# Second half's model-dimension product by seven block products, and another written order of the pieces around it

## The chip, the cores and the metric

The kernel runs on one NeuronCore of a Trainium2 chip. The metric is device time in microseconds of one execution, as the median of runs. The engines that matter here are TensorE (PE in the profile; weight loads are PEld), VectorE (DVE), ScalarE (ACT), GpSimd (POOL), and SyncE (SP), which only issues transfers here; GpSimd issues transfers too. Data live in SBUF, which the kernel cuts into pages, in PSUM, where matmuls add up, and in device memory.

## The reference, cut to what matters

```python
def _A_ref(x, dft_seq_re, dft_seq_im, dft_hid_re, dft_hid_im):
    a = jnp.einsum("bsd,ed->bse", x, dft_hid_re)
    b = jnp.einsum("bsd,ed->bse", x, dft_hid_im)
    return jnp.einsum("ts,bse->bte", dft_seq_re, a) - jnp.einsum("ts,bse->bte", dft_seq_im, b)

def _B_ref(x, w1, w2):
    h = jnp.einsum("bsd,df->bsf", x, w1)
    h = _silu(h)
    return jnp.einsum("bsf,fd->bsd", h, w2)

h = x + _A_ref(_layernorm(x, axis=-1), A_dft_seq_re, A_dft_seq_im, A_dft_hid_re, A_dft_hid_im)
h2 = h + _B_ref(_layernorm(h, axis=-1), B_w1, B_w2)
```

The sequence has 2048 positions, the model dimension is 512, the hidden one of the feed-forward part 1792, all in float32. So there are two big kinds of products in the first part, along the sequence (2048 by 2048) and along the model dimension (512 by 512), each with a real and an imaginary matrix, and two in the second part.

## The kernel before, in words

Each float32 operand is split into a rounded high part and a remainder, and each product is made of three matmuls, high by high, high by remainder, remainder by high (`three`, lines 199 to 203). The splitting is the preparation: ScalarE rounds (line 151), VectorE subtracts (line 155, or 157 where the operand changes its sign); `rounded` returns the first and leaves the second to be called later.

The kernel takes the sequence product first, because the two dimensions commute, in two halves of the output (q = 0, 1) and with two matrices (c = 0 real, 1 imaginary): `plain(0, 0)`, `fast(1, 0)`, then `mix(0)` along the model dimension, then `fast(0, 1)`, `fast(1, 1)`, `mix(1)`, then the feed-forward part, `up` and `down`, for each half. `fast` (line 543) is a product by seven block products, Strassen's scheme in Winograd's form: matrices cut into 2 by 2 blocks, sums of blocks on the operands, seven products in place of eight, sums of the products. Its product n is worked over four chunks `jj`, 12 matmuls each. The order is 1, 3, 2, then 6, 5, 7 and 4 in turns. `after1` to `after3` (lines 565 to 575) copy finished products out of PSUM on ScalarE, `post` (line 614) adds products up on VectorE. `mix(q)` (line 674) is not by seven products: for each c and each of two halves i of the model dimension and two pieces tau of the output, one step of 24 matmuls with the weights `hid`, which are loaded, rounded and used in each half anew. At its end `add_y` adds the result to the input, `h`, and `store_h` and `norm_h` follow.

All work is written as pieces with a time: `step` puts a block of matmuls at the planner's clock, which counts 0.2265 us a matmul, its preparations at that time less a lead (`LOAD_US` 18 for loads, `PREP_US` 8 for remainders, 2.2 more for the rounding), and what follows it at its end; `at` places other pieces. `program` returns the pieces sorted by these times, and they are written in that order. For the engines in `ORDERED` (PE, DVE, ACT and POOL) the order of writing is held with `issue_after`; the place of SyncE's transfers among themselves is left to the framework. The times are thus an order on each engine, not times at which something starts: an instruction starts when its engine reaches it and its inputs and its output's space are there. A page of SBUF (51 of them, 4 KB a partition) is given to each new tile by `Plan.places`, which takes, in the order of writing, the page whose last use is planned to end first. A load into a page waits for that use.

The sums of the second weights, `make_w2` (line 943), and of the first, `sums_w1` (line 811), are prepared during the first part and kept in device memory, from where `fetch_w2` and `fetch_w1` bring them back.

Of the kernel before, what the change touches and what calls it, by code (L numbers as in the profile page):

```python
# [7 lines left out]
F32 = mybir.dt.float32  # L8
# [59 lines left out]
class Plan:  # L68
# [64 lines left out]
def program(nc, page, keep, small, psum, dram, x, xT, seq, hid, ffn, out):  # L133
# [83 lines left out]
    def at(t, f):  # L217
        events.append((t, 1, len(events), f))
# [113 lines left out]

    cd = [dram.tile([2, 2, P, 2, 512], F32, name=f"cd{q}") for q in range(2)]

    def store_c(q, i, tau):
        nc.gpsimd.dma_start(cd[q][i, tau], C.pop((0, q, i, tau)))

    def load_c(q, i, tau):
        t = C[0, q, i, tau] = page(f"c{q}{i}{tau}")
        nc.sync.dma_start(t, cd[q][i, tau])  # L340

    def begin(keys):

# [34 lines left out]
    def plain(c, q):  # L378
# [154 lines left out]
            step(12, lambda n=n, jj=jj: prod(n, jj), before, after)  # L533
        at(clock[0] + 8, ready)
        for n, v in enumerate(((0, 0), (1, 0), (1, 1), (0, 1))):
            at(clock[0] + 8 + 1.2 * n, lambda v=v: store_c(q, *v))
# [6 lines left out]
    def fast(c, q):  # L543

        A = {1: (0, 0), 2: (0, 1), 3: ("S", 4), 4: (1, 1), 5: ("S", 1), 6: ("S", 2), 7: ("S", 3)}
        B = {1: (0, 0), 2: (1, 0), 3: (1, 1)}

        def mul(n, jj, on=False):
            hi, lo = part.pop(("A", c, q, n, jj))
            w = X[(*A[n], jj)]  # L550
            for m in range(2):
                for a in range(2):
                    d = slice(m * P, (m + 1) * P)
                    three(acc[c, q, n][:, m, :], w[:, 0, a, d], w[:, 1, a, d], hi[:, a, :], lo[:, a, :],
                          jj == JJ[0] and a == 0 and not on, jj == JJ[-1] and a == 1, on)

        kept = {}

        def copy_out(n, name):
            t = kept[name] = page(f"{name}{c}{q}")  # L560
            for m in range(2):
                nc.scalar.activation(t[:, m, :], acc[c, q, n][:, m, :], AF.Copy)
            return t

        def after1():
            copy_out(1, "p1")
            acc[c, q, 2] = acc[c, q, 1]

        def after2():
            C[c, q, 0, 0] = copy_out(2, "c11")  # L570
            acc.pop((c, q, 1)), acc.pop((c, q, 2))

        def after3():
            copy_out(3, "p3")
            acc.pop((c, q, 3))

        for n in (1, 3, 2):
            for jj in JJ:
                key = ("A", c, q, n, jj)

                def mm(n=n, jj=jj):
                    if n != 2 and jj == JJ[0]:
                        acc[c, q, n] = banks(f"m{c}{q}{n}")
                    mul(n, jj, on=n == 2)

                last = jj == JJ[-1]
                step(12, mm, [(LOAD_US, lambda n=n, jj=jj, key=key: load_seq(c, q, jj, *B[n], key)),
                              *halves(PREP_US, lambda key=key: round_raw(key))],
                     [(0, {1: after1, 2: after2, 3: after3}[n])] if last else ())

        def sub(o, a, b):
            nc.vector.tensor_tensor(o, a, b, op=ALU.subtract)  # L592

        B4 = {}

        def load(jj):
            for k, tau in ((0, 1), (0, 0), (1, 1)):
                load_seq(c, q, jj, k, tau, ("B", k, tau))
                B4[k, tau, jj] = raw.pop(("B", k, tau))

        def prep(n, jj):

            b11, b12, b22 = (B4[k + (jj,)] for k in ((0, 0), (0, 1), (1, 1)))
            o = {5: b11, 7: b12, 6: b22, 4: b22}[n]
# [7 lines left out]
            raw["A", c, q, n, jj] = o  # L612

        def post(n):
            if n == 6:
                u2 = kept["p1"]
                nc.vector.tensor_tensor(u2, u2, acc.pop((c, q, 6)), op=ALU.subtract)
                nc.vector.tensor_tensor(kept["p3"], kept["p3"], u2, op=ALU.add)
            elif n == 5:
                t = C[c, q, 0, 1] = kept.pop("p3")  # L620
                nc.vector.tensor_tensor(t, acc[c, q, 5], t, op=ALU.add)
            elif n == 7:
                u3 = kept["p1"]
                nc.vector.tensor_tensor(u3, acc.pop((c, q, 7)), u3, op=ALU.add)
                t = C[c, q, 1, 1] = page(f"c22{c}{q}")
                nc.vector.tensor_tensor(t, acc.pop((c, q, 5)), u3, op=ALU.add)
            else:
                t = C[c, q, 1, 0] = kept.pop("p1")
                nc.vector.tensor_tensor(t, acc.pop((c, q, 4)), t, op=ALU.add)

        for n, j in ((6, 0), (5, 0), (7, 0), (6, 1), (4, 0), (5, 1), (7, 1), (6, 2), (4, 1), (5, 2), (7, 2), (6, 3), (4, 2),
                      (5, 3), (7, 3), (4, 3)):
            jj = JJ[j]

            def mm(n=n, jj=jj):
                if jj == JJ[0]:
                    acc[c, q, n] = banks(f"m{c}{q}{n}")
                mul(n, jj)

            before = halves(ADD_US[1] if n == 4 else PREP_US, lambda k=("A", c, q, n, jj): round_raw(k))  # L640
            if n == 4:
                before.append((ADD_US[0], lambda jj=jj: prep(4, jj)))
            elif n == 6:
                before += [(PREP_US + 2 * GAP_US + d, lambda jj=jj, m=m: prep(m, jj)) for d, m in ((2.4, 5), (1.2, 7), (0, 6))]
                before.append((LOAD_US + 2.4, lambda jj=jj: load(jj)))
            step(12, mm, before, [(0, lambda n=n: post(n))] if jj == JJ[-1] else ())
        if c == 0:
            t = clock[0]
            for i, tau, d in ((0, 0, 0), (0, 1, 2), (1, 0, 8), (1, 1, 8)):
                at(t + d, lambda i=i, tau=tau: store_c(q, i, tau))  # L650


    H, y, h = {}, {}, {}
# [2 lines left out]
        raw["H", c, i] = page(f"hid{c}{i}")  # L656
        nc.sync.dma_start(raw["H", c, i], hid[c, i].rearrange("p (m e) -> p m e", m=2))

    def load_h(q, tau):
        for e in range(2):  # L660
            t = h[q, tau, e] = page(f"h{q}{tau}{e}")
            nc.sync.dma_start(t, xT[2 * tau + q][:, 2 * e : 2 * e + 2, :])

    hd = [dram.tile([2, 2, P, 2, 512], F32, name=f"hd{q}") for q in range(2)]

# [4 lines left out]
    def store_h(q, tau):  # L670
        for e in range(2):
            nc.gpsimd.dma_start(hd[q][tau, e], h[q, tau, e])

    def mix(q):
        for c in range(2):
            for i in range(2):
                for tau in range(2):

                    def round_h(c=c, i=i):
                        H[c, i], remainder = rounded(raw.pop(("H", c, i)), f"H{c}{i}")  # L680
                        return remainder

                    def round_c(tau=tau, c=c, i=i):
# [3 lines left out]

                    def mm(tau=tau, c=c, i=i):
                        hi, lo = part.pop(("M", q, tau, c, i))
                        wh, wl = H[c, i] if tau == 0 else H.pop((c, i))  # L690
# [9 lines left out]
                    if tau == 0:  # L700
                        before = [(LOAD_US, lambda c=c, i=i: load_hid(c, i)), *halves(PREP_US, round_h)] + before
                    if c == 0:
                        before.append((LOAD_US - 1, lambda i=i, tau=tau: load_c(q, i, tau)))
                    if c == 1 and i == 1:
                        before.append((LOAD_US - 6, lambda tau=tau: load_h(q, tau)))
                        after = [(0, lambda tau=tau: add_y(q, tau)), (0.5, lambda tau=tau: store_h(q, tau))]
                    step(24, mm, before, after)
        for tau in range(2):
            norm_h(q, tau, clock[0] + NORM_US[q][tau])
# [431 lines left out]
    for _ in range(WARM):  # L1141
        nc.tensor.matmul(idle[:, 0, :], warm[:, :P], warm, start=True, stop=True)  # L1142

    return sorted(events, key=lambda v: v[:3])


# [32 lines left out]
```

## Time and profile before

| | |
|---|---|
| median of 3 runs | 676.83 us (676.39 to 676.86) |
| profiled execution, its span | 674.5 us |
| TensorE, VectorE, ScalarE, GpSimd busy | 669.2, 556.7, 351.0, 92.0 us |
| matmuls | 2940 |
| transfers | 177.01 MB, 262 GB/s over the span |
| granted clock of TensorE | 1.00 |

The profile is one execution on the chip. Its span runs from the first to the last instruction; the time of a run has some 2.3 us more around it. A line like L155 is a line of the kernel, and `out<-in` names tiles. In rows of groups the numbers after the count are busy time, mean duration of one in ns, and idle time of the engine just before, with what ended it. Where one helper makes all roundings, they share its line, and the tile's name tells them apart: `raw` and `ph`, `pl` for sequence matrices, `c` for the sequence product's result, `hid` and `H..` for the model matrices, `T` for the operands of `up`.

### The profile page before, as it was taken

The page shows a single profiled execution, that of the slowest core. Times are in us where ns is not written, and L with a number is a line of the kernel's source. Part 1 is how long each engine was busy: PE and PEld are TensorE (multiplying, and loading weights), DVE is VectorE, ACT ScalarE, POOL GpSimd, SP SyncE. Part 2 cuts the span into 40 slices and gives each one's busy share as a digit, 9 for nine tenths or more (in the row PEclk, how much of TensorE's full clock was granted, in tenths as well). Part 3 has the DMA queues.
Part 4 walks back from the last instruction along what each step waited for, and adds up shares of the span by engine and source line. Part 5 has one row for each costly group of instructions (what it writes and reads, how often), then busy time and mean ns, then how long its engine had stood idle before and what let it go on. Part 6 is the DMA issues. An engine that isn't in the chain of part 4 may idle for free.

```text
span 674.5 us, 8322 instructions
## 1 busy us (share of the span) xinstructions
PE 669.2 (99%) x2940; PEld 551.2 (82%) x2940; DVE 556.7 (83%) x705; ACT 351.0 (52%) x445; POOL 92.0 (14%) x114
## 2 busy tenths in 40 slices
PE   9999999999999999999999999999999999999997
PEld 6888888888888888888888888888888888888886
DVE  7899999988646899989899989657999555549984
ACT  6789747544422544364454626556654545565510
POOL 0011211110000241123120304511100000000000
PEclk9999999999999999999999999999999999999999
DMA  8968999976599467987799995537997676467702
GB/s 315 397 211 175 310 374 368 274 206 227 188 356 332 166 156 187 339 315 236 219 264 403 414 419 188 197 99 269 387 409 249 214 272 243 187 249 282 280 33 93
DMA packets 58010, 177.01 MB, mean 262 GB/s; under 512 B 6512, under 2 KB 14192, under 8 KB 57968
## 3 DMA queue, kind: packets, MB, share of 16 engines
q1 hardware_dynamic: 44880, 131.09, 53.9%
q0 software_dynamic: 12800, 45.12, 22.2%
q8 instruction: 23, 0.38, 0.2%
q10 hardware_dynamic: 288, 0.26, 0.1%
q14 instruction: 19, 0.16, 0.1%
HBM read 137.63 MB, written 38.81 MB: 262 GB/s over the span
## 4 chain that ended last, share of the span: by engine, by line
PE 99%; DVE 0%; ACT 0%; issue 0%
PE m L202 11%; PE m L201 11%; PE m L203 11%; PE y L201 8%; PE y L203 8%; PE y L202 8%; PE f L203 6%; PE f L201 6%; PE f L202 6%; PE c L203 4%; PE c L201 4%; PE c L202 3%; PE vx L201 3%; PE vx L203 3%; PE vx L202 3%; PE idle L1142 1%
## 5 line engine op out<-in xcount | busy, mean ns | idle before, releaser
L151 ACT ACTIVATE ph<-raw 128x1024 fp32r<-128x1024 f32 x102 | 104.0, 1052 | 106.7 <-DVE raw L592 36.5
L155 DVE TENSOR_TENSOR pl<-raw,ph 128x1024 fp32r<-128x1024 f32 x100 | 124.5, 1258 | 15.0 <-ACT ph L151 14.4
L201 PE MATMUL m<-ph,S 128*128 128x512 f32 x192 | 74.7, 389 | 0.0
L202 PE MATMUL m<-pl,S 128*128 128x512 f32 x192 | 74.7, 389 | 0.0
L203 PE MATMUL m<-ph,S 128*128 128x512 f32 x192 | 74.7, 389 | 0.0
L878 DVE TENSOR_TENSOR g<-vx,g 128x512 f32<-128x512 f32 x42 | 28.8, 688 | 53.6 <-PE vx L203 24.3
L201 PE MATMUL f<-gth,wf 128*128 128x512 f32 x161 | 62.6, 389 | 0.0
L202 PE MATMUL f<-gtl,wf 128*128 128x512 f32 x161 | 62.6, 389 | 0.0
L203 PE MATMUL f<-gth,wf 128*128 128x512 f32 x161 | 62.6, 389 | 0.0
L151 ACT ACTIVATE gth<-g 128x1024 fp32r<-128x1024 f32 x42 | 43.2, 1055 | 36.1 <-DVE g L995 35.0
L203 PE MATMUL m<-ph,X 128*128 128x512 f32 x144 | 56.0, 389 | 0.0
L202 PE MATMUL m<-pl,X 128*128 128x512 f32 x144 | 56.0, 389 | 0.0
L201 PE MATMUL m<-ph,X 128*128 128x512 f32 x144 | 56.0, 389 | 0.0
L155 DVE TENSOR_TENSOR gtl<-g,gth 128x1024 fp32r<-128x1024 f32 x42 | 50.9, 1218 | 2.1 <-ACT gth L151 1.9
L592 DVE TENSOR_TENSOR raw<-raw,raw 128x1024 f32<-128x1024 f32 x36 | 47.5, 1320 | 0.9 <-DMA raw<-in_seq 0.4
L203 PEld LDWEIGHTS m<-ph,S 128*128 128x128 f32 x192 | 36.1, 188 | 7.5
L201 PEld LDWEIGHTS m<-ph,S 128*128 128x128 f32 x192 | 36.0, 188 | 7.5
L202 PEld LDWEIGHTS m<-pl,S 128*128 128x128 f32 x192 | 36.0, 188 | 7.4
L875 ACT ACTIVATE g<-y 128x512 f32<-128x512 f32 x42 | 25.0, 597 | 30.9 <-PE y L203 29.9
L872 ACT ACTIVATE g<-g 128x512 f32<-128x512 f32 x42 | 26.3, 627 | 19.1 <-DVE g L878 19.1
L202 PEld LDWEIGHTS f<-gtl,wf 128*128 128x128 f32 x161 | 30.2, 188 | 6.3
L203 PEld LDWEIGHTS f<-gth,wf 128*128 128x128 f32 x161 | 30.2, 188 | 6.3
(277 smaller groups left out, 1543.7 us busy)
## 6 DMA issues: line engine op xcount, KB each, us to landing
raw<-in_seq SPq DMA_DIRECT2D x84, 512.0 KB, 6.5
wf<-wd SPq DMA_DIRECT2D x56, 512.0 KB, 5.3
sf<-sd SPq DMA_DIRECT2D x28, 512.0 KB, 5.6
raw<-in_seq POOLq DMA_DIRECT2D x16, 512.0 KB, 5.9
w<-in_ffn SPq DMA_DIRECT2D x28, 256.0 KB, 6.1
hid<-in_hid SPq DMA_DIRECT2D x8, 512.0 KB, 4.5
c<-cd SPq DMA_DIRECT2D x8, 512.0 KB, 5.1
h<-in_xT SPq DMA_DIRECT2D x8, 512.0 KB, 7.3
```

The lines of the kernel that those rows point to most:

```text
L151: nc.scalar.activation(hi, src, AF.Copy, scale=sign)
L155: nc.vector.tensor_tensor(lo, src, hi, op=ALU.subtract)
L201: nc.tensor.matmul(acc, wh, mh, start=first, stop=False, skip_group_check=on)
L202: nc.tensor.matmul(acc, wh, ml, start=False, stop=False, skip_group_check=on)
L203: nc.tensor.matmul(acc, wl, mh, start=False, stop=last, skip_group_check=on)
L592: nc.vector.tensor_tensor(o, a, b, op=ALU.subtract)
L872: nc.scalar.activation(g[q, f][:, tau, :], src, AF.Silu)
L875: nc.scalar.activation(g[q, f][:, tau, :], src, AF.Copy)
L878: nc.vector.tensor_tensor(g[q, f][:, tau, :], src, g[q, f][:, tau, :], op=ALU.add)
L1142: nc.tensor.matmul(idle[:, 0, :], warm[:, :P], warm, start=True, stop=True)
```

## The change

`mix(0)` stays as it is, but keeps its loaded `hid` tiles, and besides makes the sums of blocks for the seven products, rounds them and stores them in device memory (`sums_hid`, `round_sums`, `store_hid`, `store_a11`), in high and remainder parts. `mix(1)` is replaced by `mix_fast(1)`: seven products of two steps (c = 0, 1) of 12 matmuls, in the order 1, 7, 6, 2, 5, 4, 3, with the weights fetched back (`fetch_hid`), and operands that are sums of the sequence products' blocks (`sum_c`). For that the two sequence products of the second half end in other forms (`forms`): product 6 is added, with its sign changed, onto product 1's bank, after ScalarE has copied product 1 into a second bank, which product 2 goes on from; and `post_forms` makes four sums where `post` makes six.

SyncE joins `ORDERED`. And a table, `MOVED`, adds a shift to the planned time of 868 of the 1500 pieces, which are numbered in the order in which `program` makes them: 488 go back, 380 forward, by 5.84 us in the median and up to 46.5. No block of matmuls is among them.

```diff
-ORDERED = (mybir.EngineType.PE, mybir.EngineType.DVE, mybir.EngineType.Activation, mybir.EngineType.Pool)
+MOVED = {
+    0: -89.72, 1: -73.79, 2: -66.91, 3: -18.04, 4: -26.92, 5: -20.32, 6: -29.82, 7: -14.98, 8: -9.18, 11: -10.08,
...
+    424: -3.85, 426: -37.86, 427: 1.24, 428: -0.93, 430: -11.59, 431: -6.37, 432: -4.29, 434: -37.27, 435: -5.11,
+    436: -6.38, 438: 9.361, 439: -14.48, 440: -4.66, 441: 1.22, 444: -2.03, 445: -0.38, 447: 6.67, 448: -1.11,
...
+    580: 0.92, 582: 12.19, 583: -2.739, 584: -2.033, 585: 0.206, 587: 9.65, 588: 6.5, 589: 6.03, 591: -5.47,
...
+    703: -8.44, 704: 1.08, 705: -8.517, 706: -6.38, 708: 1.9, 709: 1.31, 710: -10.864, 713: 23.6, 714: -22.41,
...
+    789: 18.27, 790: -23.55, 791: -5.72, 792: 3.41, 793: 15.67, 794: 3.865, 795: 2.91, 796: 22.62, 797: -31.31,
+    798: -27.74, 799: 40.61, 800: 41.64, 801: -6.38, 802: -5.89, 803: 38.77, 804: -41.83, 805: -34.9, 806: -4.215,
...
+    835: -4.115, 836: 5.4, 837: 3.23, 839: 7.73, 840: 13.41, 841: 0.55, 842: 0.43, 843: -1.74, 844: 0.36, 845: 2.78,
+    846: 4.71, 847: 10.5, 848: 13.85, 849: 11.68, 850: -46.51, 851: 5.86, 852: 3.09, 853: 4.52, 861: 5.2, 862: 3.79,
...
+}
+ORDERED = (
+    mybir.EngineType.PE, mybir.EngineType.DVE, mybir.EngineType.Activation, mybir.EngineType.Pool, mybir.EngineType.SP,
+)
...
-        kept = {}
+        kept, forms = {}, q == 1
...
         def after1():
-            copy_out(1, "p1")
-            acc[c, q, 2] = acc[c, q, 1]
+            if not forms:
+                copy_out(1, "p1")
+                acc[c, q, 2] = acc[c, q, 1]
+                return
+            acc[c, q, 6], acc[c, q, 2] = acc.pop((c, q, 1)), banks(f"m{c}{q}2")
+            for m in range(2):
+                nc.scalar.activation(acc[c, q, 2][:, m, :], acc[c, q, 6][:, m, :], AF.Copy)
...
+        def post_forms(n):
+            if n == 6:
+                copy_out(6, "u2")
+                acc.pop((c, q, 6))
+            elif n == 7:
+                t = C[c, q, 7] = kept.pop("p3")
+                add(t, acc[c, q, 7], t, ALU.subtract)
+                add(kept["u2"], acc.pop((c, q, 7)), kept["u2"])
+                t = C[c, q, 3] = page(f"c22{c}{q}")
+                add(t, acc.pop((c, q, 5)), kept["u2"])
+            elif n == 4:
+                t = C[c, q, 2] = kept.pop("u2")
+                add(t, acc.pop((c, q, 4)), t)
...
+    def sums_hid(c):
+        a, b = (raw.pop(("H", c, i)) for i in range(2))
+        a11, a21, a12, a22 = a[:, :, :256], a[:, :, 256:], b[:, :, :256], b[:, :, 256:]
+        s = [page(f"hs{c}{n}", F32, (2, 2, 256)) for n in range(2)]
+        s1, s3, s2, s4 = s[0][:, 0], s[0][:, 1], s[1][:, 0], s[1][:, 1]
+        for o, x, y, op in ((s1, a21, a22, ALU.add), (s3, a11, a21, ALU.subtract), (s2, s1, a11, ALU.subtract), (s4, a12, s2, ALU.subtract)):
+            nc.vector.tensor_tensor(o, x, y, op=op)
+        made_h[c] = s
...
+    def store_hid(c, n):
+        for m, t in enumerate(made_h.pop((c, n)) if n < 2 else H[c, 1]):
+            nc.gpsimd.dma_start(fd[c][2 * n + m], t.bitcast(F32).rearrange("p f m e -> p f (m e)") if n < 2 else t.bitcast(F32))
+
+    def store_a11(c):
+        for m, t in enumerate(H[c, 0]):
+            nc.gpsimd.dma_start(ad[c][m], t.bitcast(F32)[:, :, :256])
+
+    def fetch_hid(c, n):
+        t = [page(f"hf{c}{n}{m}", F32, (2, 2, 256) if n < 2 else (2, 512) if n == 2 else (2, 256)) for m in range(2)]
+        for m in range(2):
+            o = t[m].rearrange("p f m e -> p f (m e)") if n < 2 else t[m]
+            nc.sync.dma_start(o, fd[c][2 * n + m] if n < 3 else ad[c][m])
...
+    def mix_fast(q):
...
+        def sum_c(c, n):
+            o = page(f"t{c}{n}")
+            x, y, op = {6: (7, 1, ALU.add), 5: (3, 6, ALU.subtract), 4: (2, 6, ALU.subtract)}[n]
+            add(o, C[c, q, x], C[c, q, y], op)
+            C[c, q, n] = o
...
+        def mm(n, c):
+            if c == 0 and n in (1, 7):
+                bank[n] = banks(f"y{q}{n}")
+            elif c == 0:
+                bank[n] = bank[{6: 1, 5: 6, 3: 5, 4: 7, 2: 2}[n]]
+            fresh = n in (1, 7)
+            hi, lo = part.pop(("M", q, c, n))
+            wh, wl = H[c, n]
+            for e in range(2):
+                for m in range(2):
+                    s = slice(e * P, (e + 1) * P)
+                    three(bank[n][:, e, :], wh[:, m, s], wl[:, m, s], hi[:, m, :], lo[:, m, :],
+                          fresh and c == 0 and m == 0, c == 1 and m == 1, not fresh)
+
+        def seed():
+            bank[2] = banks(f"y{q}2")
+            nc.scalar.activation(bank[2], bank[1], AF.Copy)
...
+        after = {
+            1: [(0, seed)],
+            7: [(0, lambda: copy_out(7)), (1.5, lambda: residual(1, 1, kept.pop(7)))],
+            6: [(0, lambda: copy_out(6)), (1.5, lambda: residual(0, 1, kept.pop(6)))],
+            2: [(0, lambda: residual(0, 0, bank[2]))],
+            5: [(0, lambda: copy_out(5)), (1.5, lambda: residual(1, 1, kept.pop(5)))],
+            4: [(0, lambda: residual(0, 1, bank[4])), (0.5, lambda: store_h(q, 0))],
+            3: [(0, lambda: residual(1, 0, bank[3])), (0.5, lambda: store_h(q, 1))],
+        }
+        order = (1, 7, 6, 2, 5, 4, 3)
...
+                step(12, lambda n=n, c=c: mm(n, c), before, after[n] if c else ())
...
-    mix(1)
+    mix_fast(1)
...
-    return sorted(events, key=lambda v: v[:3])
+    return sorted(((t + MOVED.get(n, 0.0), at, n, f) for t, at, n, f in events), key=lambda v: v[:3])
```

More of the change, by code (lines that the diff above doesn't have):

```diff
@@ L635, in mm @@
             def mm(n=n, jj=jj):
-                if jj == JJ[0]:
+                on = forms and n == 6
+                if jj == JJ[0] and not on:
                     acc[c, q, n] = banks(f"m{c}{q}{n}")
-                mul(n, jj)
-            before = halves(ADD_US[1] if n == 4 else PREP_US, lambda k=("A", c, q, n, jj): round_raw(k))
+                mul(n, jj, on)
+            sign = -1.0 if forms and n == 6 else 1.0
+            before = halves(ADD_US[1] if n == 4 else PREP_US, lambda k=("A", c, q, n, jj), sign=sign: round_raw(k, sign))
             if n == 4:
@@ L657, in load_hid, with load_h @@
         nc.sync.dma_start(raw["H", c, i], hid[c, i].rearrange("p (m e) -> p m e", m=2))
[L659 to L662, printed above, removed]
+    def load_h(q, tau, e):
+        t = h[q, tau, e] = page(f"h{q}{tau}{e}")
+        nc.sync.dma_start(t, xT[2 * tau + q][:, 2 * e : 2 * e + 2, :])
     hd = [dram.tile([2, 2, P, 2, 512], F32, name=f"hd{q}") for q in range(2)]
@@ L672, in store_h @@
             nc.gpsimd.dma_start(hd[q][tau, e], h[q, tau, e])
+    fd = [dram.tile([6, P, 2, 512], F32, name=f"fd{c}") for c in range(2)]
+    ad = [dram.tile([2, P, 2, 256], F32, name=f"ad{c}") for c in range(2)]
+    made_h = {}
+    def sums_hid(c):
[6 more added lines that the diff above has]
+        made_h[c] = s
@@ new lines, in round_sums @@
+    def round_sums(c, n):
+        made_h[c, n], remainder = rounded(made_h[c][n], f"hS{c}{n}", shape=(2, 2, 256))
+        return remainder
+    def store_hid(c, n):
[4 more added lines that the diff above has]
+            nc.gpsimd.dma_start(ad[c][m], t.bitcast(F32)[:, :, :256])
```

83 lines of the change are left out of this document (69 added, 14 removed), and 86 rows, old and new, of the table MOVED.

## The prediction

> **What bounds the kernel now.** I read the page's first and fourth parts, then the waits of TensorE, then its timeline at both ends, then busy times by stage.
>
> ```profile
> span 674.5 us, 8322 instructions
> PE 669.2 (99%) x2940; PEld 551.2 (82%) x2940; DVE 556.7 (83%) x705; ACT 351.0 (52%) x445; POOL 92.0 (14%) x114
> PE 99%; DVE 0%; ACT 0%; issue 0%
> PE idle L1142 <- DVE upper L1135: 1.2, 1, 1.2
> 1.18 5.26 PE L1142 MATMUL idle<-warm 128*128 128x512 bf16 x12 [1.18 <-DVE upper L1135]
> 5.92 1.45 PE L396 MATMUL c<-ph,X 128*128 128x512 f32 x4
> 670.02 0.39 PE L203 MATMUL f4b<-gth,wf 128*128 128x512 f32 x1
> ```
>
> The chain that ended last is TensorE all along. Its view of waits has one row, the start before the warm-up. Of 2940 matmuls 12 are that warm-up, so 2928 do work; from the first start to the last there are 2927 steps in 670.02 - 5.92 = 664.1 us, which is 0.2269 us a step with everything in it. Nothing else is on the path: a matmul taken out is worth 0.227 us, and any wait that a changed order puts before a matmul is paid in full, since no later slack of TensorE's swallows it.
>
> **The product by seven blocks.** `mix(1)` runs 8 steps of 24 matmuls, 192; `mix_fast(1)` runs 14 steps of 12, 168. The sequence products keep their number (product 6 goes into product 1's bank, no matmul more). So 24 go: 24 x 0.2269 = 5.44 us. Their shape (128x512 moving, 128x128 stationary) stays. The 669.1 us span that is left, with the 676.83 - 674.5 = 2.3 us that the median has around the profiled span, would be 671.4 us. Only if nothing waits does it count, so the rest is a search for waits.
>
> ```profile
> 164.00:207.00 43.00, 43.00 (x192) 35.59 (x191) 26.75 (x29) 13.30 (x14) 3.72 (x7) 1.00 0.78 280
> 207.00:284.00 77.00, 77.00 (x341) 63.76 (x340) 66.56 (x71) 32.74 (x36) 17.02 (x16) 1.00 0.75 224
> 284.00:360.00 76.00, 76.00 (x337) 62.93 (x336) 70.78 (x76) 37.66 (x41) 18.05 (x18) 1.00 0.86 275
> 360.00:403.00 43.00, 43.00 (x191) 35.60 (x190) 40.61 (x46) 20.63 (x21) 7.40 (x14) 1.00 1.03 412
> 403.00:488.00 85.00, 85.00 (x376) 70.38 (x375) 65.61 (x103) 50.96 (x77) 24.02 (x22) 1.00 0.65 229
> 353.15 1.22 DVE L155 TENSOR_TENSOR pl<-raw,ph 128x1024 fp32r<-128x1024 f32 x1
> 354.29 1.22 DVE L155 TENSOR_TENSOR H00l<-hid,H00h 128x1024 fp32r<-128x1024 f32 x1
> L301 DVE TENSOR_TENSOR s<-xc,xc 128x512 f32<-128x512 f32 x4 | 2.7, 682 | 0.0
> ```
>
> The rows are stretches: length, then busy time of PE, weight loads, DVE, ACT and POOL, the granted clock, DMA share and GB/s. They are the first half's model product (164 to 207), the second half's two sequence products (to 284 and to 360), the model product in question (to 403) and the first `up` with the beginning of `down`. The two timeline rows give VectorE's pitch: a 128x1024 operation starts 1.14 us after the one before, though it lasts 1.22.
>
> *VectorE.* In the stage: remainders 14 in place of 12 (8 of the sequence result, 4 of `hid`), six `sum_c`, six residuals in place of four sums: 10 operations more, 11.4 us at 1.14. In each of the two sequence products `post_forms` has 4 sums where `post` has 6: 2.3 us less each. In the first half's model product, `sums_hid` and `round_sums` are 8 operations of 512 and 4 of 1024: 8 x 0.68 + 4 x 1.22 = 10.3 us, and that stretch has 43 - 26.75 = 16.2 us free. That part is free.
>
> The stretch from 284 to 403 isn't. VectorE is busy for 70.78 + 40.61 = 111.4 of 119 us. With -2.3 + 11.4 it needs 120.5 us in a stretch that has shrunk to 113.6: 6.9 us too much, unless pieces leave it. Their takers are on both sides: 77 - 66.56 = 10.4 us free before it and 85 - 65.61 = 19.4 us after it. The shift table does move pieces there. I numbered the pieces as the program makes them and added the shifts: loads of `w2` for 4, 3 and 2 move up by 42, 31 and 24 us (804, 797, 790), and the residual of product 6 moves back by 24 (713), behind the first steps of `up`. From the planned start of the second sequence product of this half to the stage's end, 113 us, I count 114.7 us of VectorE by row durations, which is 114.7 x 1.14/1.22 = 107 us at the pitch: it fits, with 6 us over. Cost: nothing while data are there in time; if a third of the 6.9 us found no place, 2.3 us of late remainders.
>
> *ScalarE, POOL, SyncE.*
>
> ```profile
> L151 ACT ACTIVATE ph<-raw 128x1024 fp32r<-128x1024 f32 x102 | 104.0, 1052 | 106.7 <-DVE raw L592 36.5
> L562 ACT ACTIVATE p<-m 128x512 f32<-128x512 f32 x12 | 6.5, 594 | 10.1 <-PE m L203 8.8 <-DVE pl L155 1.3
> L1014 ACT ACTIVATE p<-f 128x1024 f32<-128x1024 f32 x10 | 10.0, 1023 | 3.9 <-PE f L203 3.5 <-DMA wf<-wd 0.3
> L672 POOL DMA_DIRECT2D hd<-h x8 | 4.3, 532 | 29.9 <-DVE h L668 29.9
> L657 SPq DMA_DIRECT2D hid<-in_hid x8: 327/330/1440, 142.5 to 365.3; - x8
> raw<-in_seq SPq DMA_DIRECT2D x84, 512.0 KB, 6.5
> ```
>
> ScalarE gets 2 roundings more, a seed and 3 copies in the stage, 2 x 1.05 + 4 x 1.02 = 6.2 us against 43 - 20.63 = 22.4 free; 1.2 us in each sequence product (two copies of 0.594); 4.2 us in the first half's stage, which has 29.7 free. A copy from one PSUM bank into another does not occur in the trace. Bounds: 0.59 us, as L562's smaller read, and 2.0, twice L1014; I take L1014's 1.02, the nearest. In program order a product of four steps (4 x 12 x 0.2269 = 10.9 us) lies between product 1 and the one that needs the seed. But `after1` of the third sequence product is moved back by 9.36 us (438), so it stands 1.5 us ahead of its reader, and the rounding of earlier loads is queued before it on ScalarE: a load that is late there stops TensorE at the seed. POOL gets 16 stores, 8.5 us of issue, in 43 - 3.72 = 39.3 free; behind them wait the accumulating loads and the norm's reductions, which have leads of several us. SyncE has 16 fetches for 4 loads, 12 x 0.33 = 4.0 us of issue.
>
> The transfers: fetches bring 14 x 0.524 = 7.3 MB where 2.1 came, 5.2 MB more between 284 and 403, where 76 us at 275 GB/s and 43 at 412 are 20.9 + 17.7 = 38.6 MB. 43.9 MB in 113.6 us is 386 GB/s, under the 412 that the row for 360 to 403 shows. The stores (7.3 MB on top of 43 x 280) overflow the first half's stage and drain before 284, where 224 GB/s leave room. I take nothing for it. The Trainium skill, "DMA: Bandwidth & Descriptors", section "Where 436 GB/s comes from", says that transfers between HBM and SBUF are bound near 358 GB/s per core; by that the 43.9 MB would take 122.6 us, 9 too long. The 412 of this trace is above it, so the trace does not agree; a rival below keeps a small chance for it.
>
> *SyncE in the written order, pieces elsewhere.* The table shifts 868 of 1500 pieces, no matmul. A raw tile's way is load, 6.5 us to landing, 1.05 us, 1.22 us: 8.8 us. By plan the load stands 18 us ahead of its matmuls: 9.2 us to spare. The table cuts this in places. The load of block (2,3) of the last sequence product goes back by 9.65 (587): 8.35 us ahead, half a us short if it were issued only then. The remainder of T5, the first `up`'s fifth operand, goes back by 13.41 (840), from 15.1 to 1.7 us ahead of its matmuls. The numbers are an order, not times, and a queue that is free runs ahead, so this may cost nothing; the bounds are a few us at each end (below, nothing but tenths, as TensorE has no wait to lose; above, the 2 to 8 us of the rivals). I put 0.3 us for all of it: 674.5 - 5.4 + 0.3 = 669.4 span, **671.7 us**.
>
> **The rivals.**
>
> ```profile
> SPq L327 <- PE m L203: 52.2, 14, 7.6
> SPq L327 <- DVE pl L155: 36.0, 15, 6.1
> SPq L327 <- DVE S L294: 13.7, 2, 13.4
> ```
>
> *Small waits at several places.* VectorE's saturated stretch and the thinned leads (T5, the seed) each give up some tenths to 2 us. For it: 6.9 us had to find another place, and nothing after TensorE absorbs a wait. Against: the count above leaves 6 us. With the third named, 671.4 + 2.3 = 673.7 us.
>
> *SyncE blocked at one tile: slower.* Loads wait for the page they overwrite, and these rows say how long the queue stood for raw tiles: up to 7.6 us for a matmul, 13.4 once. Now the order is fixed while pages are asked for up to 46 us earlier, so one such wait stands ahead of loads like (2,3) with nothing to spare. A 7.6 us stand there costs 7.6 + 0.5 = 8.1 us, and the restart would be slow if the clock falls: the 12 warm-up matmuls took 5.26 us, 0.438 each, against 0.227, so 12 at that pace are 2.5 us more. 671.4 + 8.1 + 2.5 = 682.0 us. It decides from 5.4 + 1.4 = 6.8 us of wait on. Against: pages are planned by uses in that very order, and every raw tile of the trace waited like that without TensorE waiting. The Trainium skill, "TensorE: Matmul & The Clock Gate", Part 1, says that the clock halves after an idle window of some 3.4 us and needs as long to come back, which would be about 1.7 us in place of my 2.5; the granted clock here is 1.00 in every row, so no idle of that length is shown.
>
> *Transfers become the bound.* With the rate per share of the 403 to 488 row, 229/0.65 = 352 GB/s at full share, 43.9 MB take 124.7 us where there are 113.6: 671.4 + 11.1 = 682.5 us. Against: 412 in the stage itself.
>
> *The change does not do what it says*: excluded, as the count of matmuls follows from the loops.
>
> **How the numbers follow.** Nothing or under 0.8 us of waits: 0.50, which is the forecast. Small waits up to 4 us: 0.28. Waits that eat the gain: 0.07. SyncE blocked 0.12, transfers 0.03. About 0.2%, 1.35 us, is what a measurement of this kernel tells from no change. Faster than 675.5: 0.50 + 0.28 = 0.78; within: 0.07; slower than 678.2: 0.15. The likeliest case alone spans 670.9 to 672.2. The range starts at 670.8, 0.6 us under the sum without waits, for tenths of waits that the 0.2269 may hold and a start that may come earlier, and must reach into the waits until a fifth is left out: 677.0.
>
> **What would show it.** Right: 2916 matmuls in all, pitch 0.227, no row of waits beside the start, VectorE over 94% busy from 284 to 398, DMA near 390 GB/s there with share about 1. Wrong: TensorE waiting for fetched `hf` tiles or, through their roundings, for `raw` behind SyncE; for `pl` or `T5l` behind VectorE; for the seed behind ScalarE; a granted clock under 1.00; or a pitch that changes with the strided weights of the fetched forms, which I take to be none.

## The result, and the profile after

| | before | after |
|---|---|---|
| median of runs | 676.85 us (676.39 to 677.85, 4 runs) | 671.21 us (671.13 to 671.33, 4 runs) |
| ratio, 95% interval | | 0.9914, 0.9900 to 0.9928 |
| profiled execution: its time, its span | –, 674.5 us | 671.13, 669.3 us |
| matmuls | 2940 | 2916 |
| transfers | 177.01 MB | 189.59 MB |

The kernel became 5.6 us faster. These are the first and fourth parts of the page of after, the one row of TensorE's view of waits, and the last matmul.

```profile
span 669.3 us, 8342 instructions
PE 663.7 (99%) x2916; PEld 546.7 (82%) x2916; DVE 571.2 (85%) x723; ACT 365.8 (55%) x459; POOL 98.8 (15%) x130
PE 99%; DVE 0%; ACT 0%; issue 0%
PE idle L1392 <- DVE upper L1385: 1.2, 1, 1.2
664.53 0.39 PE L302 MATMUL f4b<-gth,wf 128*128 128x512 f32 x1
```

TensorE is still the whole chain and still waits for nothing but the start. The last matmul starts at 664.53 in place of 670.02, 5.49 us earlier; 24 steps of 0.2269 are 5.44. In both kernels neighbouring matmuls start 0.22667 us apart in a stretch without waits (0.2267 below); all that lies above this pitch, added up from the first matmul at 5.92 to the last, is 0.64 us before and 0.59 after. So nothing the change adds reached TensorE. What it used up is seen in the windows of after (columns as in the prediction: length, then PE, weight loads, DVE, ACT, POOL, granted clock, DMA share, GB/s), the last three of them finer:

```profile
164.00:207.00 43.00, 43.00 (x191) 35.59 (x191) 33.25 (x34) 18.21 (x18) 9.36 (x17) 1.00 0.88 308
207.00:284.00 77.00, 77.00 (x342) 63.75 (x341) 70.56 (x75) 35.89 (x39) 22.76 (x20) 1.00 0.84 290
284.00:360.00 76.00, 76.00 (x337) 62.94 (x336) 70.81 (x82) 38.98 (x43) 14.09 (x17) 1.00 0.99 336
360.00:398.00 38.00, 38.00 (x170) 31.45 (x169) 37.13 (x36) 23.47 (x24) 2.65 (x5) 1.00 0.89 336
340.00:360.00 20.00, 20.00 (x90) 16.57 (x89) 18.57 (x22) 10.31 (x11) 1.95 (x3) 1.00 1.04 379
360.00:380.00 20.00, 20.00 (x90) 16.57 (x89) 19.20 (x20) 12.81 (x13) 2.12 (x4) 1.00 0.98 386
380.00:398.00 18.00, 18.00 (x82) 14.88 (x81) 17.93 (x17) 10.66 (x11) 0.53 (x1) 1.00 0.79 280
```

Three resources are at or near their limit together from 284 to 398: TensorE at 114.00 of 114 us, VectorE at 70.81 + 37.13 = 107.9 (95%), the DMA engines, which carry the transfers, at a share near 1 until 380. In the last 38 us VectorE is at 37.13. Its timeline there, and the weight loads of the tile that it makes last for the first `up`, show how near that is:

```profile
398.98 0.95 DVE L393 TENSOR_TENSOR wal<-w,wah 128x768 fp32r<-128x768 f32 x1
399.85 1.22 DVE L848 TENSOR_TENSOR h<-61_3307,h 128x1024 f32<-128x1024 f32 x1
400.99 1.22 DVE L1045 TENSOR_TENSOR hn<-hn,hn 128x1024 f32<-128x1024 f32 x1
402.12 1.22 DVE L254 TENSOR_TENSOR T5l<-hn,T5h 128x1024 fp32r<-128x1024 f32 x1
403.26 1.21 DVE L848 TENSOR_TENSOR h<-y,h 128x1024 f32<-128x1024 f32 x1
L301 PEld LDWEIGHTS y<-T5l,sf x28: 187/188/188, 403.6 to 594.7; 128*128 128x128 f32 x28
```

VectorE works without a gap, one operation every 1.14 us. The remainder of T5 ends at 402.12 + 1.22 = 403.34, and its first weight load starts at 403.6: 0.3 us to spare.

Smaller things that the prediction named, from the views by tile and SyncE's waits:

```profile
L300 PE MATMUL y<-ph,hf x56: 389/389/389, 360.1 to 397.5; 128*128 128x512 f32 x56
L675 ACT ACTIVATE m<-m x4: 577/580/582, 227.2 to 296.6; 128x512 f32<-128x512 f32 x4
L880 ACT ACTIVATE y<-y x1: 1007/1007/1007, 366.9 to 366.9; 128x1024 f32<-128x1024 f32 x1
229.56 0.39 PE L300 MATMUL m<-ph,X 128*128 128x512 f32 x1
SPq L426 <- DVE pl L254: 51.1, 13, 14.6
```

The fetched, strided forms `hf` cost a matmul nothing: 389 ns, least, median and most, and nothing above the pitch is lost between 130 us and the last matmul. Copies from one PSUM bank into another, the seeds, occur in two places: two of 0.58 us in each sequence product of the second half, one of 1.007 us for twice the size in `mix_fast`. In the third sequence product the first product-2 matmul starts at 229.56, about 1.2 us after the second copy. SyncE stood up to 14.6 us for the page of one raw tile (L426), twice the 7.6 of the SyncE rival, and TensorE did not notice.

### The profile page after: what moved, and what is told of

Read it like the earlier page. It is cut to its first block, busy times and chain, and to the rows that moved or that the text cites. A ratio compares the mean times of both kernels' runs of the same rounds, so it can differ in the third digit from the quotient of the medians.

```text
span 669.3 us, 8342 instructions
## 1 busy us (share of the span) xinstructions
PE 663.7 (99%) x2916; PEld 546.7 (82%) x2916; DVE 571.2 (85%) x723; ACT 365.8 (55%) x459; POOL 98.8 (15%) x130
## 2 busy tenths in 40 slices
DMA packets 61786, 189.59 MB, mean 283 GB/s; under 512 B 6960, under 2 KB 14640, under 8 KB 61744
## 4 chain that ended last, share of the span: by engine, by line
PE 99%; DVE 0%; ACT 0%; issue 0%
PE m L302 11%; PE m L301 11%; PE m L300 11%; PE y L302 8%; PE y L301 8%; PE y L300 8%; PE f L301 6%; PE f L300 6%; PE f L302 6%; PE c L302 4%; PE c L300 4%; PE c L301 4%; PE vx L301 3%; PE vx L302 3%; PE vx L300 3%; PE idle L1392 1%
## 5 line engine op out<-in xcount | busy, mean ns | idle before, releaser
L254 DVE TENSOR_TENSOR pl<-raw,ph 128x1024 fp32r<-128x1024 f32 x92 | 113.9, 1256 | 6.9 <-ACT ph L250 5.7
L300 PEld LDWEIGHTS f<-gth,wf 128*128 128x128 f32 x161 | 30.2, 188 | 6.3
L302 PEld LDWEIGHTS f<-gth,wf 128*128 128x128 f32 x161 | 30.2, 188 | 6.3
```

The lines of the kernel that those rows point to most:

```text
L254: nc.vector.tensor_tensor(lo, src, hi, op=ALU.subtract)
L300: nc.tensor.matmul(acc, wh, mh, start=first, stop=False, skip_group_check=on)
L302: nc.tensor.matmul(acc, wl, mh, start=False, stop=last, skip_group_check=on)
```

## Experiments

Times are medians; the ratio is to the kernel before, on the same chip. "Lost" is the time from the first to the last matmul of a stage above 0.2267 us a step; after itself loses 0.59 us over all of them. Beside the different runs the kernel before took 676.5 to 676.9 us, so some tenths between two runs tell nothing. e6 and e13 leave part of the result out.

| run | median us (lowest to highest) | ratio, 95% interval |
|---|---|---|
| e1_sp_free | 674.93 (674.32–677.38) | 0.9978, 0.9962–0.9993 |
| e2_no_moves | 710.03 (707.78–711.84) | 1.0488, 1.0461–1.0514 |
| e3_seven_alone | 710.40 (709.38–714.70) | 1.0507, 1.0472–1.0542 |
| e4_before_sp | 676.35 (676.09–676.54) | 0.9993, 0.9984–1.0003 |
| e5_t5_twice | 672.39 (672.28–672.67) | 0.9939, 0.9925–0.9952 |
| e6_without_3 | 672.12 (671.83–673.15) | 0.9937, 0.9923–0.9951 |
| e7_traffic | 689.73 (688.93–690.39) | 1.0194, 1.0180–1.0208 |
| e8_sums_twice | 677.62 (677.49–678.13) | 1.0014, 1.0005–1.0023 |
| e10_first_stage | 687.74 (686.14–689.40) | 1.0162, 1.0143–1.0181 |
| e12_third_traffic | 677.78 (674.85–678.10) | 1.0006, 0.9995–1.0017 |
| e13_without_3_all | 670.55 (669.35–671.12) | 0.9902, 0.9885–0.9918 |
| e14_seven_two_kept | 708.62 (707.28–710.38) | 1.0469, 1.0446–1.0492 |

### The order: SyncE and the table

**e1_sp_free** and **e4_before_sp** take SyncE's written order away from after, and give it to before.

```diff
 ORDERED = (
-    mybir.EngineType.PE, mybir.EngineType.DVE, mybir.EngineType.Activation, mybir.EngineType.Pool, mybir.EngineType.SP,
+    mybir.EngineType.PE, mybir.EngineType.DVE, mybir.EngineType.Activation, mybir.EngineType.Pool,
 )
```

> The changed kernel, with SyncE's transfers left to the framework's order again; the table of shifts stays. Theory (the 24 matmuls are the gain, 5.44 us, and all of the order work serves to keep waits at nothing): the shifts of loads lose their hold, so TensorE may wait, 671.2 to 676. Rival (SyncE's written order is a risk that brings nothing): 671.2, as with it. Second rival (the gain comes from the order of the transfers): 676 or more.

> The kernel before, with SyncE in the written order and nothing else changed. Theory (the planned order was already close to what the framework chose, and leads of 18 us leave 9 us to spare): 676.8, within 1 us. Rival (a queue held at one tile blocks the loads behind it): 680 to 690, with TensorE waiting in the profile.

Without it after takes 674.93 us, 3.7 more, lost in small waits in many places, all for VectorE. The three largest of the five rows of TensorE's view of waits in e1 that lie behind the start, all for remainders, as are the other two (0.4 and 0.2 us):

```profile
PE y L301 <- DVE T5l L254: 0.9, 1, 0.9
PE y L302 <- DVE H11l L254: 0.6, 1, 0.6
PE m L301 <- DVE pl L254: 0.5, 1, 0.5
```

On before, with its old times, the same switch moves nothing that can be measured.

**e2_no_moves** and **e3_seven_alone** empty the table; e3 also leaves SyncE free, so that of the change the seven products alone remain.

```diff
-MOVED = {
-    0: -89.72, 1: -73.79, 2: -66.91, 3: -18.04, 4: -26.92, 5: -20.32, 6: -29.82, 7: -14.98, 8: -9.18, 11: -10.08,
...
-}
+MOVED = {}
```

> The changed kernel with an empty table of shifts; SyncE stays in the written order. Theory: 24 matmuls fewer give 671.2, and VectorE, which needs 6.9 us more than the stretch from 284 to 398 has, makes TensorE wait for some 2 to 7 us: 673 to 678. Rival 1 (the shifts are not needed): 671.2 to 671.7. Rival 2 (SyncE held at one tile blocks what stands behind it, and it is the shifts that avoid it): 680 or more, with rows of TensorE waiting for what depends on loads.

> The seven block products alone: an empty table of shifts, and SyncE's transfers left to the framework. Theory: as the run with an empty table, 673 to 678, since what is late is VectorE. Rival 1 (shifts not needed): 671.2 to 671.7. Rival 2 (a SyncE in the written order is what hurts without shifts): clearly under the run with SyncE in the written order, by 3 us or more.

Both take 710 us, 39 more than after; both theories missed by more than 30. The number of e2's second rival came true, but e3 shows that SyncE's place in the order is not the reason. SyncE's order has no effect without the table (710.03 and 710.40). The largest rows of TensorE's waits in e3:

```profile
PE m L205 <- DVE pl L158: 10.3, 8, 4.3
PE y L204 <- ACT g L1029: 6.6, 2, 4.6
PE y L204 <- DMA hf<-fd: 4.3, 1, 4.3
```

Lost in all: 41.0 us, of which 2.4 in `plain` and 3.8 in the first `fast`, which the change does not touch; 10.0 in the sequence product behind `mix(0)`, 10.8 in `mix_fast`, 9.8 behind it.

**e14_seven_two_kept** asks for the early part. The pieces of `make_w2` for the first two parts are placed from the clock at the end of the first part, which now ends 24 matmuls earlier; so the planner puts them 5.4 us earlier into `plain` and `fast`. Here e3 has these pieces back in their old places:

```diff
-        make_w2(clock[0] + t, p)
+        make_w2(clock[0] + (24 * MM_US if p < 2 else 0) + t, p)
```

> The seven products alone (empty table, SyncE left to the framework), with the first two preparations of the second weights (p = 0 and 1) put back to the planned time that they had before; the shorter clock had moved them 5.4 us forward against the pieces around them. In the run of the seven products alone TensorE lost 6.2 us before any new work begins (2.4 in the first product, 3.8 in the second), of 41 in all. Theory (those 6.2 come from that displacement): they vanish, 704 us. Rival (they come from somewhere else in the change): 710 again.

The loss in `plain` and the first `fast` falls from 6.2 to 0.9 us, so the shifted pieces were its cause. The medians differ by 1.8 only, and the ranges overlap: the stages behind lose 3.1 us more in the profiled execution, and the run (708.62) misses its time. A form with all seven parts moved (e9) gave no time.

**e10_first_stage** has before's second half and, of the new work, only what the first half's model product gets: the sums, their roundings and the stores. Nothing fetches them; no shifts, SyncE free.

```diff
+MOVED = {}
...
-        kept, forms = {}, q == 1
+        kept, forms = {}, False
...
-    mix_fast(1)
+    mix(1)
```

> The kernel before, with only the new work of the first half's model product: sums of the model matrices' blocks, their rounding and 16 stores, which nothing fetches; the second half as before, no shifts. The prediction had this part as free (10.3 us of VectorE where 16.2 are free). Theory 1 (free): 676.7, within 0.7. Theory 2 (the 10 us that TensorE lost in the next sequence product, in the runs without shifts, come from this work in the planned order, since the free time lies elsewhere in the stretch): 685 to 692.

687.74 us, 11 more than before: this new work is not free in the old order. Where the 8.9 us that the next sequence product loses come from is read in e10's windows, in the timelines of ScalarE and TensorE, and in SyncE's waits from 195 to 240:

```profile
207.00:230.00 23.00, 21.75 (x96) 17.35 (x95) 18.95 (x17) 10.42 (x11) 6.17 (x12) 1.00 0.99 378
223.94 1.09 ACT L569 ACTIVATE p<-m 128x512 f32<-128x512 f32 x2 [3.79 <-DMA fd<-H11h]
232.40 2.01 ACT L154 ACTIVATE ph<-raw 128x1024 fp32r<-128x1024 f32 x2 [6.22 <-DMA raw<-in_seq]
242.09 0.80 PE L205 MATMUL m<-pl,X 128*128 128x512 f32 x1 [4.30 <-DVE pl L158]
SPq L330 <- DMA fd<-hS11h: 6.6, 1, 6.6
```

VectorE has 4 us free in that stretch. The stores fill the transfers (share 0.99), the copy `p` waits 3.79 us for the page that a store reads, and the loads of the sequence matrices land late: ScalarE waits 6.22 us for one, and TensorE 4.30 us for the remainder made of it. SyncE's queue, which issues these loads, stands 6.6, 6.3, 6.1 and 2.2 us for pages that four of the stores still read. So most of the 8.9 us goes back to the stores: 4.5 at the late remainder and 2.4 of slow clock behind it. How much is the held page and how much the full DMA engines is not told apart, and no run has the sums without the stores; 0.8 us at the stage's start is a wait for VectorE's `h`.

### VectorE's reserve

**e5_t5_twice** makes T5's remainder of the first half of `up` twice, **e8_sums_twice** each of the six `sum_c`.

```diff
-            return remainder
+            return (lambda: (remainder(), remainder())) if (q, n) == (0, 5) else remainder
```

```diff
             add(o, C[c, q, x], C[c, q, y], op)
+            add(o, C[c, q, x], C[c, q, y], op)
```

> The changed kernel, in which VectorE makes the remainder of T5 for the first up twice over, 1.14 us more at that place. In the changed kernel's trace that remainder ends at 402.12 + 1.22 = 403.34 and its first weight load starts at 403.64: 0.30 us to spare. Theory (VectorE sets the pace there and a wait is paid in full): 1.14 - 0.30 = 0.84 us more, 672.05. Rival (the written order leaves room, queues run ahead of it): nothing, 671.2.

> The changed kernel with each of the six sums of sequence blocks in the stage made twice over by VectorE, 6 x 1.14 = 6.8 us more between 334 and 370. Theory (the stretch has next to nothing left: 0.3 us at T5, and VectorE busy 107.9 of 114): 3 to 6.5 us of waits, and up to 2.5 more where a wait lets the clock fall: 674 to 680. Rival (6 us are over in the stretch, as the count of the prediction had it): within 1 us of 671.2.

e5 is 1.2 us slower than after. 1.14 us of work on a reserve of 0.3 is 0.84; lost behind `mix_fast`: 0.91. The profiled execution loses another 0.6 near 120 us, in the first `fast`, where after loses some tenths too; the edit does not touch that place, and why is open. The row of the wait in e5:

```profile
PE y L301 <- DVE T5l L254: 0.6, 1, 0.6
```

e8 adds six operations, 6.8 us at the pitch, and is 6.4 us slower. Its rows between 284 and 420:

```profile
PE y L301 <- DVE pl L256: 2.5, 2, 1.8
PE y L301 <- DVE T5l L254: 0.9, 1, 0.9
PE m L301 <- DVE pl L254: 0.7, 1, 0.7
```

Nearly all of the added work is paid for: 6.2 us are lost from the last sequence product on, 5.0 of them at remainders due before T5 and 1.2 at T5. So T5 is not the only tile with next to nothing to spare. If 6 us had been over, it would have cost about 1 us.

**e6_without_3** turns the question round: product 3's 24 matmuls are left out, VectorE's work stays.

```diff
         def mm(n, c):
...
+            if n == 3:
+                return
```

> The changed kernel without the matmuls of product 3 of the second half's model product (24 fewer again); all preparation, transfers and sums stay, so part of the result is left out. Rival (TensorE alone sets the end, a matmul is 0.227 us anywhere): 671.2 - 5.4 = 665.8. Theory (after the change VectorE is as tight as TensorE in this stretch): T5's remainder has 0.3 us to spare, so TensorE gets to it 5.4 us early and waits about 5; little or nothing is gained, 670.5 to 672.5, with TensorE waiting for VectorE around 398 and perhaps a slower clock behind it.

24 matmuls fewer bring nothing: 672.12 us, 0.9 more than after. From e6's view of waits, a window, and TensorE's timeline:

```profile
PE y L302 <- DVE wal L393: 2.1, 1, 2.1
PE y L300 <- ACT wah L1099: 0.5, 1, 0.5
392.00:412.00 20.00, 17.35 (x63) 13.41 (x62) 19.64 (x21) 10.13 (x15) 4.21 (x8) 0.83 0.75 282
397.18 0.63 PE L300 MATMUL y<-T1h,wah 128*128 128x512 f32 x1
402.30 0.61 PE L300 MATMUL y<-T6h,sf 128*128 128x512 f32 x1
```

VectorE, at 19.64 of 20 us, now sets the end of this stretch. TensorE waits for it, and then the granted clock falls: between the two rows shown lie twelve steps of (402.30 - 397.18) / 12 = 0.427 us in place of 0.227, 2.4 us more. Of the 6.1 us lost between 390 and 410, against 5.4 saved, some 3 are such slow steps, 2.3 the wait for VectorE's `wal` and 0.7 the one for ScalarE's `wah`. By these numbers the waits alone would have left about 2 of the 5.4 us (an estimate).

**e13_without_3_all** also leaves out product 3's preparation and residual.

```diff
         def round_c(c, n):
+            if n == 3:
+                part["M", q, c, n] = None, None
+                return lambda: None
...
+            if n == 3:
+                return
...
-            3: [(0, lambda: residual(1, 0, bank[3])), (0.5, lambda: store_h(q, 1))],
+            3: [(0, lambda: None), (0.5, lambda: store_h(q, 1))],
```

> As the run without product 3's matmuls, but without its preparation too: two roundings, two remainders and the residual, 3 x 1.14 = 3.4 us less for VectorE; part of the result is left out. Theory (VectorE is the second bound of this stretch): T5's remainder comes 3.4 us earlier, with the 0.3 to spare the gain is up to 3.7 of the 5.4 us, 667.5 to 669. Rival (what TensorE waits for there is transfers or ScalarE): 670.5 or more. Second rival (TensorE alone): 665.8.

670.55 us: 0.7 less than after, where 2 to 4 were expected; the rival for transfers or ScalarE had named 670.5 or more. The profiled execution, 671.12, is the slowest of four; the two whose granted clock was 1.00 took 669.35 and 670.10, 1.1 to 1.9 less than after. Of the three operations taken from VectorE one lay in the gapless run that ends with T5's remainder; of the others one lay ahead of it, where VectorE still waits now and then, and one behind it. VectorE also waited 0.29 and 0.44 us for roundings of ScalarE's on the way (at 379.02 and 389.89), so ScalarE has a share in the missing gain. The timelines of VectorE and of TensorE in e13:

```profile
400.84 1.22 DVE L254 TENSOR_TENSOR T5l<-hn,T5h 128x1024 fp32r<-128x1024 f32 x1
402.12 0.50 PE L301 MATMUL y<-T5l,sf 128*128 128x512 f32 x1 [2.07 <-DVE T5l L254]
403.65 0.63 PE L301 MATMUL y<-T1l,wah 128*128 128x512 f32 x1
406.64 0.54 PE L302 MATMUL vx<-T2h,wal 128*128 128x512 f32 x1
```

T5's remainder starts 1.28 us earlier than in after (400.84 for 402.12), but TensorE stands ready at 402.12 - 2.07 = 400.05, over 3 us earlier than there. So it waits again, and again runs at half the clock afterwards (seven steps in 406.64 - 403.65 = 2.99 us).

### The transfers' reserve

**e7_traffic** puts a copy of 0.52 MB, from device memory to device memory, behind each of twelve fetches on SyncE's queue, 6.3 MB; **e12_third_traffic** four of them, 2.1 MB.

```diff
             nc.sync.dma_start(o, fd[c][2 * n + m] if n < 3 else ad[c][m])
+            if n < 3:
+                nc.sync.dma_start(more[c][2 * n + m], fd[c][2 * n + m])
```

> The changed kernel, in which SyncE, behind each fetch of model sums, also copies the same 0.52 MB within device memory, 12 times, 6.3 MB more between 284 and 398, where 38.3 MB move in 114 us; 391 GB/s with it. Theory (transfers are not the bound, 412 was reached): 671.2 to 672. Rival (transfers are at their limit there, so that loads come late): 675 or more, TensorE waiting for what depends on raw or hf.

> As the run with more traffic, but 4 copies in place of 12: 2.1 MB more in the stretch. There 6.3 MB cost 18.5 us, about what they take at 350 to 390 GB/s. Theory (transfers have almost nothing left in this stretch, each further MB is paid at some 2.6 us): 671.2 + 3 to 6 us = 674 to 677. Rival (there is room, and only the larger number fell over an edge, with the slow clock behind long waits): under 672.

In e7 my theory fell and its rival came true: it is 18.5 us slower than after. e12 is 6.6 slower, 0.8 above its theory's range. That is 2.9 and 3.1 us for each MB. Part of e12's 6.6 is the clock: the profiled execution loses 3.1 us at a fetch and 2.4 in slow steps behind it, and two executions with a granted clock of 0.999 and 1.00 took 674.85 and 675.77. e7's wait, windows and fetches, and a window of e12 (the last row):

```profile
PE y L300 <- DMA hf<-fd: 10.7, 1, 10.7
340.00:360.00 20.00, 19.39 (x86) 15.74 (x85) 17.71 (x22) 10.19 (x11) 1.95 (x3) 1.00 1.07 379
360.00:380.00 20.00, 18.10 (x79) 14.22 (x77) 14.35 (x13) 7.99 (x8) 1.59 (x3) 1.00 0.99 395
380.00:400.00 20.00, 8.09 (x20) 5.91 (x21) 9.07 (x11) 5.44 (x6) 0.53 (x1) 0.57 0.85 345
L834 SPq DMA_DIRECT2D hf<-fd x12: 319/320/332, 327.7 to 381.6; - x12
360.00:380.00 20.00, 17.11 (x77) 13.88 (x75) 19.21 (x20) 12.82 (x13) 2.13 (x4) 1.00 1.03 417
```

The DMA engines are full in all three kernels: shares of 1.07 and 0.99 in e7 from 340 to 380, 1.03 twice in e12, 1.04 and 0.98 in after. The rate at a full share is not one figure: 379 and 395 GB/s in e7, 370 and 417 in e12, 379 and 386 in after, 412 in before's stage. So what is used up in this stretch is the engines' time; a ceiling in GB/s is not shown. The last fetch is issued at 381.6; in after it is at 364.8. The copies stand in the same queue ahead of later fetches, so how much of the delay is the rate and how much the queue is not told apart.

## Why the prediction was right

**The matmuls.** 24 x 0.2269 = 5.44 us was the right term: 5.49 measured between the last matmuls.

**The sum.** The forecast span, 669.4, was measured as 669.3. Two small terms were mis-sized and a third had no place in the sum. The 0.3 us for the order was nothing (0.59 us above the pitch after, 0.64 before). What follows the last matmul grew from 674.5 - 670.02 = 4.5 to 669.3 - 664.53 = 4.8 us, which I did not follow up. And the 2.3 us around the span is 671.13 - 669.3 = 1.8: I had taken the median of the runs less the span of one execution. That is the half microsecond between 671.7 and 671.21.

**"A wait is paid in full".** Right, and too low where the clock falls with it (e6, e13, e7, e12).

**"With 6 us over" on VectorE.** The count was right, 114 - 107.9 = 6.1 us idle, and what it was taken to mean was wrong. The share came out as expected (95% where "over 94%" was named), but the reserve at T5 is 0.3 us, one more operation there is paid (e5), and six more ahead of it cost 6.4 of 6.8 us (e8). The step that failed is to read idle time, added up over 113 us, as a reserve: by the windows of after 5.2 of the 6.1 us lie before 360, and they do not help the remainders due behind. That after did not pay for this was luck in part: 0.3 us were left.

**"That part is free" in the first half's stage.** The time of VectorE is there, as said; what failed is the stores, which "overflow the first half's stage and drain before 284". In after 14 of the 16 are issued before 207, among shifted loads; in the old order they delay the loads of the next product, and the stage's new work costs 11 us (e10).

**The transfers, "I take nothing for it".** Right in the result, for another reason. I worked out 386 GB/s from 284 to 398; measured is 336 over the stretch, 336 x 114 = 38.3 MB, where 43.9 had been counted. The fetches did add their 5.2 MB; what I left out is that other transfers leave the stretch. Of the second weights' stores (`wd`) 16 are issued there before and 8 after, 4.2 MB less, and of the sequence loads 20 and 18, 1.0 MB less. One of the four kinds of these stores, from the views of transfers of before (284 to 403) and after (284 to 398):

```profile
wd<-Uh POOLq DMA_DIRECT2D x4, 512.0 KB, 8.5
wd<-Uh POOLq DMA_DIRECT2D x2, 512.0 KB, 9.4
```

Had these 5.2 MB stayed, they would have cost some 15 us at the 3 us for each MB of e12 and e7: an estimate, as the copies of those runs also stood in the queue ahead of fetches. The Trainium skill, "DMA: Bandwidth & Descriptors", section "Where 436 GB/s comes from", puts the limit between HBM and SBUF near 358 GB/s; the 386 of after between 360 and 380 is above that, as the 412 of before was.

**The order, "this may cost nothing".** Right in the result, and the question was put the wrong way. I searched the table for damage; its main effect is that it makes the seven products worth anything: 39 us lie between after and the same products without it (e2, e3). It is not the source of the gain: before lost 0.64 us in all between its first and its last matmul, so no order could have gained more than that there without fewer matmuls. Of the 41 us lost in e3 some 5 stand in the first stages, where the shorter clock pulled `make_w2` (e14; taken away, part of it came back further on), some 10 in the product behind the stores' stage (e10 shows it without the rest), and most of the rest in `mix_fast` and behind it, not taken apart. Three pieces (0 to 2) are moved by more than the 46.5 us named with the change, by 67 to 90.

**The rivals.** *Small waits* did not happen in after, but e1 shows them with SyncE free: 674.93, all for VectorE. *SyncE blocked* was priced by the wrong number: SyncE stood 14.6 us and nothing was late. What counts would then be the lead of the loads behind it and not the stand; that is my reading, no run holds SyncE longer. *Transfers as the bound* was nearer than its 3%: 2.1 MB more, in the same queue, were enough to take the gain (e12: 1.0006, 0.9995 to 1.0017).

**The seed** of `mix_fast` took 1.007 us where I had 1.02, those of the sequence products 2 x 0.58 = 1.16 where I had 1.2; the one of the third sequence product, put 1.5 us ahead of its reader, kept 1.2. T5's lead, put at 1.7 us, came down to 0.3.

## What to carry to other kernels

When one engine is at 99%, look at what the second and third resource have free in that very stretch, at each tile that is due there: it bounds what work taken from the first can bring. Here the first 24 matmuls brought their full 5.4 us and the next 24 nothing, in part because the clock fell behind the new waits. Pieces that are placed by a clock move when the clock gets shorter, in stages that the change does not touch, so the order around the change belongs to its price. And a count of an engine's free time doesn't show whether a page, a store or a queue delays the next stage's loads.

## What the runs showed of the hardware

**The clock can fall after a wait of 2 us, and need not.** TensorE ran at 0.427 us a step after waits of 2.07 (e13, for some 3.4 us) and 2.11 us, with one of 0.54 just ahead (e6, for 5.5 us), and kept its clock after one of 1.8 us (e8, granted clock 1.00 in its windows). The length of the wait does not decide it: at the same matmul e3 and e14 wait 2.02 and 2.03 us, and the clock falls in e14 alone (first the row and a window of e3, then those of e14).

```profile
434.62 0.50 PE L204 MATMUL y<-T6h,sf 128*128 128x512 f32 x1 [2.02 <-ACT g L1029]
432.00:441.00 9.00, 6.98 (x31) 5.47 (x30) 8.90 (x10) 2.87 (x4) 2.81 (x4) 1.00 1.00 361
430.91 0.50 PE L204 MATMUL y<-T6h,sf 128*128 128x512 f32 x1 [2.03 <-ACT g L1029]
428.00:439.00 11.00, 8.97 (x33) 6.87 (x31) 10.90 (x10) 2.87 (x4) 4.52 (x4) 0.84 0.96 344
```

In e3 even a wait of 3.19 us (at 120.99) left the granted clock at 1.00 from 116 to 127, and of e13's four executions only two show a lower clock. Nor does the fall come at one moment: in e13 the slow steps begin 1.5 us after the wait's end, in e6 within 0.6. The Trainium skill, "TensorE: Matmul & The Clock Gate", Part 1, gives an idle window of about 3.4 us, free-running, ahead of the fall, and as long to come back. The length of the slow phase in e13 fits that, and a free-running window would also explain why the same wait can end either way; the waits ahead of the falls in e13 and e14 are shorter than the window.

**A copy from PSUM to PSUM** on ScalarE takes 0.58 us for 128x512 and 1.007 for 128x1024, about as much as one into SBUF (0.594 for 128x512 in the profile before).

**Transfers** at a share near 1 moved 370 to 417 GB/s over 20 us (after, e7, e12); what decides the rate was not looked into.
